# Attention x products as four 64 by 64 TensorE tiles in place of block-diagonal full-array products, two groups per batch

## The chip, the cores and the metric

One Trainium2 chip, one of its cores. The metric is the device time of one execution in microseconds (us): three runs of the kernel before gave 284.06, 284.75 and 286.88, median 284.75. A core has TensorE (PE; its weight loads are listed as PEld), VectorE (DVE), ScalarE (ACT), GpSimd (POOL) and SyncE (SP), which issues most DMAs. Matmuls write PSUM, which ACT and DVE read.

## The reference

Linear attention on q, k, v of shape (8 batches, 8 heads, 576 tokens, 64), then a two-layer network with a snake activation on the 4608 x 512 result:

```python
q_s = exp(q) / sum over d            # per token and head
k_s = exp(k) / sum over tokens       # per head and d
kv  = einsum('bhsd,bhse->bhde', k_s, v)          # 64 x 64 per head
x   = einsum('bhsd,bhde->bhse', q_s, kv)         # -> x: 4608 tokens x 512
h   = x @ w_in                                   # 512 -> 2048
g   = h + sin(alpha * h)**2 / alpha
out = g @ w_out                                  # 2048 -> 512, float32
```

## The kernel before, in words

All matmuls take bf16 operands. The order of every engine's work is written out by hand (`tc.manual_schedule()`, line 54): the program order of the Python is the order on each engine.

**Layout of the attention.** A batch's 576 tokens are 64 partitions by 9 token groups (J = 9, P = 64): token = 9 p + j. A head is (i, e), i = 0..3, e = 0, 1; a tile has partition e*64 + p. The four i are taken as two halves ii (called *head pairs* below; ii holds i = ii and i = ii + 2, which are x = 0 and x = 1). `kv_mm` (line 164) makes kv of a batch with 64 x 64 TensorE tiles: 72 products of 65 columns (the 65th is the sum for the division), 36 per ii; rows are chosen by e, output partitions by x, and e chooses one of two PSUM banks. `kv_norm` (179) divides by the sums and writes `kbd`, a block-diagonal 128 x 128 matrix per (e, ii): x = 0 in the upper left block, x = 1 in the lower right, zeros elsewhere (memset, line 310); that takes two DVE multiplies of 64 partitions. q is normalised by `norm_q` (140) and transposed, by TensorE for batches 0 and 1 and by DMA after that, into `qT`, partition x*64 + d, columns ii, j, e, p.

**x products.** `attn_chunk` (228) and `attn_out` (217) multiply one 128 x 128 block of `kbd` with up to 512 columns of `qT`; the result, c = 2*ii + e, is partitions x*64 + d of xT. Per batch that is 4 blocks of 576 columns. A copy on DVE or ACT brings PSUM to `xT` (SBUF, 128 x 4 x 2560 in bf16, a ring of five token tiles).

**The network.** 4608 tokens are nine *token tiles* t of 512. `mm_h` (247) makes one *h tile* (128 of the 2048 features, 512 tokens): four products of 512 columns over c, into one PSUM bank. There are 16 h tiles, or *slots* ni, per t. `sine` (258) runs the sine on ACT and the square on ACT, POOL or DVE; `combine` (269) adds on DVE, writes G and thereby frees the PSUM bank. `mm_o` (273) makes the output, 64 products of 512 columns per t, accumulated over ni; `evac_o` (283) copies and stores it.

**Order.** Batch 0 fills the start (lines 361 to 401): load, exp, normalise, transpose, kv, x, with the first h products between. Batch 1 is made amid the output products of t = 0 (456 to 504). The ninth token group (j = 8) of batches 0 and 1 comes late: q by `late_q8` (512), transposed after slot 11 and multiplied after slot 15 of t = 1 (eight products of 64 columns). Batch 2 lies amid the output products of t = 1 (549 to 577): four products of 384 columns into banks of the h pools, then the last three groups into a tile of `ps_a`. From t = 2 on, batch b = t + 1 is made in the slots of t by `attn_back` (581): kv at slot 5, then four x steps (of 4 and 5 token groups for each ii) at slots 9, 11, 13, 15; t = 7 and 8 have no attention. kv and x of these batches share one PSUM tile of two banks, `ps_a` with one buffer, so each waits until the copy of the one before has been made. In t >= 3 about 2.6 output products of t - 1 follow every h tile (line 619); ACT does both the sine and the square there, and at the start of every t the exp of q and k of batch t + 1, with two loads of its function tables.

**Weights.** `load_win` (106) loads w_in in pieces with a cast on POOL's DMA queue: partition 64*x + d of chunk c holds row (x, c, d), line 81, in the order in which the x products leave the features.

Of the kernel before, what the change touches and what calls it, by code (L numbers as in the profile page):

```python
# [15 lines left out]
F32 = mybir.dt.float32  # L16
BF16 = mybir.dt.bfloat16
AX = mybir.ActivationFunctionType
ALU = mybir.AluOpType
# [4 lines left out]
def kernel(  # L24
# [20 lines left out]
    J = 9  # L45
    P = S // J
    nN = d_ff // 128
    MF = 512
# [23 lines left out]
    alpha_rows = singles.tile([nN, 128], F32, name="alpha_rows")  # L72
    alpha_sb = singles.tile([128, nN], F32, name="alpha_sb")
    inva_sb = singles.tile([128, nN], F32, name="inva_sb")
    kbd = [singles.tile([128, 2, 2, 128], BF16, name=f"kbd{n}") for n in range(2)]
    vb = [singles.tile([128, J, 4 * 65], BF16, name=f"vb{n}") for n in range(2)]

    def src_view(t, b):
        return t[b].rearrange("(i e) (p j) d -> (e p) i (j d)", e=2, j=J)

    win_v = moe_w_in.rearrange("(x c d) n -> x d c n", x=2, c=4)
    wout_v = moe_w_out.rearrange("(no ni) d -> ni no d", ni=128)
    out_v = out.rearrange("(b p j) d -> b j p d", b=B, j=J)

# [30 lines left out]
    A = {}  # L115
# [48 lines left out]
    def kv_mm(b, ii, pool, split=False):  # L164

        if ii == 0 or split:
            A["kvp", b] = pool.tile([128, 2, 512], F32, name="kvp", tag="a")
        kvp, ke, vt = A["kvp", b], A["ke", b], vb[b % 2]
        for j in range(J):
            for x in range(2):  # L170
                h = 2 * ii + x
                for e in range(2):
                    r = slice(64 * e, 64 * e + 64)
                    nc.tensor.matmul(kvp[64 * x:64 * x + 64, e, ii * 65:(ii + 1) * 65],  # L174
                                     ke[r, j, h * 64:(h + 1) * 64],
                                     vt[r, j, h * 65:(h + 1) * 65],
                                     start=(j == 0), stop=(j == J - 1))
# [12 lines left out]
    def q_tile(b):  # L190
        if ("qT", b) not in A:
# [23 lines left out]
    XO = ((0, 4), (4, 9))  # L215

    def attn_out(b, ii, half, pool, eng):
        qT, kt = A["qT", b], kbd[b % 2]
        j0, j1 = XO[half]
        n = (j1 - j0) * P  # L220
        xp = pool.tile([128, 2, 512], F32, name="xp", tag="a")
        for e in range(2):
            nc.tensor.matmul(xp[:, e, 0:n], kt[:, e, ii], qT[:, ii, j0:j1, e * 64:(e + 1) * 64],  # L223
                             start=True, stop=True)
        c0 = (J * b + j0) * P % NX
        eng(xT[:, 2 * ii:2 * ii + 2, c0:c0 + n], xp[:, :, 0:n])  # L226

    def attn_chunk(b, c, j0, j1, xp):

        ii, e = divmod(c, 2)  # L230
        nc.tensor.matmul(xp, kbd[b % 2][:, e, ii], A["qT", b][:, ii, j0:j1, e * 64:(e + 1) * 64],
                         start=True, stop=True)


    G = {}

# [3 lines left out]
    def bank(kind):  # L240

        if kind == "k":
            return ps_k.tile([128, 2, MF], F32, name="kvp", tag="a")[:, 0]
        pool = {"a": lambda: ps_h[0], "b": lambda: ps_h[1], "l": lambda: ps_l, "o": lambda: ps_o}[kind]()
        return pool.tile([128, MF], F32, name={"l": "lp", "o": "op"}.get(kind, "hp"), tag=kind)

    def mm_h(t, ni, k0=0, k1=4):

        if ni == 0 and k0 == 0:
            G[t] = gpool.tile([128, nN, MF], BF16, name="g")  # L250
        hp = HP[t, ni] if k0 else bank(BANKS.get(t, 4 * "aabb")[ni])
        HP[t, ni] = hp
        for ki in range(k0, k1):
            nc.tensor.matmul(hp, win[:, ki, ni * 128:(ni + 1) * 128],  # L254
                             xT[:, ki, t * MF % NX:t * MF % NX + MF], start=(ki == 0), stop=(ki == 3))
        return hp

    def sine(t, ni, hp, sq):
# [122 lines left out]
    cast_v0(1, 5, 9, DVE_CP)  # L381

    xp = [bank("b") for _ in range(2)]
    for c in range(2):
        attn_chunk(0, c, 0, 8, xp[c])
    DVE_CP(xT[:, 0, 0:MF], xp[0])
    ACT_CP(xT[:, 1, 0:MF], xp[1])
# [4 lines left out]
    for ki in range(2):  # L392
        for ni in range(2):
            mm_h(0, ni, ki, ki + 1)
    for c in range(2, 4):
        xp = bank("l")
        attn_chunk(0, c, 0, 8, xp)
        DVE_CP(xT[:, c, 0:MF], xp)
    for ki in range(2):
        for ni in range(2, 4):  # L400
            mm_h(0, ni, ki, ki + 1)
# [21 lines left out]
    def take(it, n=1000):  # L423
        for _ in range(n):
            if next(it, 0) == 0:
                return
# [4 lines left out]
    with ES:  # L431
# [47 lines left out]

        def x_half(ii):  # L480
            xp = [bank("a") for _ in range(2)]
            for e in range(2):
                attn_chunk(1, 2 * ii + e, 0, 8, xp[e])
            for e in range(2):
                (ACT_CP, DVE_CP)[e](xT[:, 2 * ii + e, MF:2 * MF], xp[e])

        kv_mm(1, 0, ps_k, split=True)
        kv_norm(1, 0, 1)
# [23 lines left out]
        def late_q8(ni):  # L512
            if ni == 11:
                tp = ps_k.tile([128, 2, 2, 128], BF16, name="tp", tag="a")
                for b in range(2):
                    for ii in range(2):
                        nc.tensor.transpose(tp[:, ii, b], A["qe", 1][:, J - 2 + b, ii * 128:(ii + 1) * 128], identb)
                DVE_CP(A["qT", 1][:, :, J - 2:J], tp)
            elif ni == 15:
                xp = ps_k.tile([128, 4, 2, P], F32, name="xp", tag="a")  # L520
                for c in range(4):
                    ii, e = divmod(c, 2)
                    for b in range(2):
                        nc.tensor.matmul(xp[:, c, b], kbd[b][:, e, ii],
                                         A["qT", 1][:, ii, J - 2 + b, e * 64:(e + 1) * 64], start=True, stop=True)
                DVE_CP(xT[:, :, 16 * P:18 * P], xp.rearrange("p c b n -> p c (b n)"))

        for ni in range(nN):
            h_slot(1, ni, SQ[ni], lag)
# [33 lines left out]
    norm_q(3, [GP])  # L563
    take(os, 20)

    c0 = J * 2 * P
# [6 lines left out]
    for c in range(4):  # L573
        attn_chunk(2, c, 6, 9, xp[:, c // 2, (c % 2) * 3 * P:(c % 2 + 1) * 3 * P])
    DVE_CP(xT[:, :, c0 + 6 * P:c0 + 9 * P].rearrange("p (h c) n -> p h c n", h=2),
           xp.rearrange("p h (c n) -> p h c n", c=2))
    take(os)
    q_transpose_dma(3)
    load_batch(4)

    def attn_back(b, n, engs=4 * (DVE_CP,), xs=(4, 6, 8, 10)):
        if n == 0:
            kv_mm(b, 0, ps_a)
            kv_mm(b, 1, ps_a)
            kv_norm(b)
        elif n in xs:
            m = xs.index(n)
            attn_out(b, m // 2, m % 2, ps_a, engs[m])

    SQ2 = "PAPPAPAPPAPAPPAP"  # L590
    for ni in range(nN):
        h_slot(2, ni, SQ2[ni], lag)
        flush(lag, 2)
        attn_back(3, ni - 5, (DVE_CP, ACT_CP, ACT_CP, DVE_CP), (4, 6, 8, 10))
    flush(lag, 0)

    for t in range(3, nT):
        b = t + 1 if t + 1 < B else None
        os = o_stream(t - 1)
        done = 0  # L600
        if b is not None:

            exp_q(b)
            exp_k(b)
            cast_v(b, [GP_CP, GP_CP])
            norm_q(b, [GP])
            take(os, 8)
            done = 8
        for ni in range(nN):
# [12 lines left out]
        take(os)  # L622
# [36 lines left out]
```

## Time and profile before

| | |
|---|---|
| median of three runs | 284.75 us |
| the profiled execution's own time | 283.85 us |
| its span, first to last instruction | 282.1 us |
| mean granted TensorE clock | 0.997 |
| PE busy | 270.1 us, 1826 matmuls recorded |
| ACT, DVE, POOL busy | 225.5, 188.7, 83.8 us |
| h products, L254 (into hp) | 127.9 us busy, x507 |
| output products, L274 (into op) | 121.6 us busy, x477 |
| kv products, L174 | 6.8 us busy, x576 |
| x products, L223 (batches 3 to 7) | 8.2 us busy, x40 |
| xT copies, L226 on DVE | 13.5 us busy, x18 |
| kbd multiplies, L187 on DVE | 7.4 us busy, x20 |

The profile is of one execution. Busy time of PE is a union of modelled intervals: a matmul's listed duration (379 ns for 512 columns) is from its start to its last result, and the next one starts before that. So the distance between starts is the price of a matmul in a stream, not its duration. A few matmul records are missing. "Idle before, releaser" after the bar in a line says how long the engine stood before these instructions and what ended it.

### The profile page before, as it was taken

Reading aid. Unit: us, or ns where it says so; the run is one execution under the profiler, and the core shown is the slowest. Engines: PE = TensorE matmul, PEld = TensorE weight load, DVE = VectorE, ACT = ScalarE, POOL = GpSimd, SP = SyncE. Lnnn points to the kernel's source line nnn. Section 1 sums busy time; section 2 is a strip of 40 time slices with the busy share of each in tenths; the row PEclk is TensorE's granted clock in tenths of the full one; section 3 lists DMA queues with packets and bytes.
Section 4 is the critical chain, followed back from the end, with each engine's and each line's share of the span. In section 5 each row is a group of like instructions: output and inputs, shape, how many; then the busy total and the mean of one; then the engine's idle time right before and its main releaser. Section 6 shows DMA issues by size and latency. Waiting matters only on the chain.

```text
span 282.1 us, 4812 instructions
## 1 busy us (share of the span) xinstructions
PE 270.1 (96%) x1826; PEld 128.0 (45%) x1855; DVE 188.7 (67%) x288; ACT 225.5 (80%) x322; POOL 83.8 (30%) x80
## 2 busy tenths in 40 slices
PE   1999999999999999999999999999999999999994
PEld 0444444444444444444444444444444444444443
DVE  3968768899967768766875677567775555555412
ACT  3989576999589999899989998999877777777400
POOL 1988421877676550115003500340000000000000
PEclk9999999999999999999999999999999999999998
DMA  7999999996599039811992099109011111111143
GB/s 252 310 173 221 280 332 322 358 345 243 124 224 393 10 68 329 305 37 38 266 386 50 22 283 388 27 18 160 6 34 37 37 40 37 37 38 43 42 104 74
DMA packets 39127, 45.80 MB, mean 162 GB/s; under 512 B 17072, under 2 KB 22464, under 8 KB 39104
## 3 DMA queue, kind: packets, MB, share of 16 engines
q1 hardware_dynamic: 33360, 40.57, 46.9%
q0 software_dynamic: 5552, 4.79, 10.4%
q8 instruction: 14, 0.23, 0.3%
q10 hardware_dynamic: 192, 0.14, 0.2%
q14 instruction: 9, 0.07, 0.1%
HBM read 36.71 MB, written 9.44 MB: 164 GB/s over the span
## 4 chain that ended last, share of the span: by engine, by line
PE 84%; DMA 6%; ACT 3%; DVE 2%; POOL 1%; issue 1%; SPq 1%; ACTq 0%
PE op L274 38%; PE hp L254 37%; DMA st_v<-in_v_dram 6%; PE xp L223 2%; PE kvp L174 2%; PE lp L254 2%; POOL s L264 1%; PE op L629 1%; PE op L254 1%; ACT s L260 1%; PE kvp L254 1%; ACT vb L329 1%; DVE g L270 1%; SPq L299 1%; SPq L445 0%
## 5 line engine op out<-in xcount | busy, mean ns | idle before, releaser
L270 DVE SCALAR_TENSOR_TENSOR g<-s,inva_sb,hp 128x512 bf16<-128x512 f32 x128 | 94.1, 745 | 58.1 <-ACT s L262 52.6
L254 PE MATMUL hp<-xT,win 128*128 128x512 bf16 x507 | 127.9, 379 | 0.4
L274 PE MATMUL op<-wout,g 128*128 128x512 bf16 x477 | 121.6, 379 | 1.4 <-issue 0.6
L260 ACT ACTIVATE s<-hp,alpha_sb 128x512 f32<-128x512 f32 x128 | 86.3, 682 | 22.9 <-PE hp L254 21.2
L254 PEld LDWEIGHTS <-win 128*128 128x128 bf16 x576 | 56.0, 98 | 67.5 <-issue 1.3
L274 PEld LDWEIGHTS <-g 128*128 128x128 bf16 x560 | 54.0, 98 | 61.0 <-DVE g L270 0.3
L262 ACT ACTIVATE s<-s 128x512 f32<-128x512 f32 x112 | 70.5, 630 | 3.5
L264 POOL TENSOR_TENSOR s<-s 128x512 f32<-128x512 f32 x29 | 30.4, 1063 | 20.0 <-ACT s L260 19.9
L153 POOL TENSOR_TENSOR qn<-qe,qs 128x1152 bf16<-128x1152 bf16 (+1 forms) x12 | 25.1, 2109 | 34.1 <-DVE qs L147 22.7
L286 DVE COPY o<-op 128x512 f32<-128x512 f32 (+2 forms) x33 | 22.1, 668 | 9.9 <-PE op L274 5.5
L138 POOL CAST vb<-st_v 128x1152 bf16<-128x1152 f32 x12 | 14.7, 1257 | 45.3 <-DMA st_v<-in_v_dram 45.3
L119 ACT ACTIVATE qe<-st_q 128x1152 bf16<-128x1152 f32 (+2 forms) x18 | 17.7, 1025 | 6.7 <-DMA st_q<-in_q_dram 6.6
L119 ACT ACTIVATE ke<-st_k 128x1152 bf16<-128x1152 f32 x16 | 17.9, 1151 | 1.2 <-DMA st_k<-in_k_dram 1.2
L146 DVE TENSOR_REDUCE qs<-qe 128x36 f32<-128x2304 bf16 x5 | 12.8, 2553 | 7.9 <-ACT qe L119 7.9
L226 DVE CAST xT<-xp 128x512 bf16<-128x512 f32 (+1 forms) x18 | 13.5, 749 | 0.0
L119 ACT ACT_TABLE_LOAD x7 | 9.0, 1283 | 1.3 <-PEq L643 1.2
L274 PE MATMUL lp<-wout,g 128*128 128x512 bf16 x31 | 8.8, 379 | 0.2 <-issue 0.2
L274 PE MATMUL hp<-wout,g 128*128 128x512 bf16 x30 | 8.6, 379 | 0.1
L223 PE MATMUL xp<-qT,kbd 128*128 128x256 bf16 (+1 forms) x40 | 8.2, 286 | 0.0
L174 PEld LDWEIGHTS <-ke 64*64 64x64 bf16 x576 | 5.8, 108 | 4.6 <-ACT ke L119 0.8
L187 DVE TENSOR_TENSOR kbd<-kvp,kvr 64x256 bf16<-64x256 f32 (+1 forms) x20 | 7.4, 369 | 0.5
L254 PE MATMUL lp<-xT,win 128*128 128x512 bf16 x30 | 7.5, 379 | 0.1
(86 smaller groups left out, 135.0 us busy)
## 6 DMA issues: line engine op xcount, KB each, us to landing
out_dram<-o SPq DMA_DIRECT2D x70, 128.0 KB, 2.4
st_q<-in_q_dram SPq DMA_DIRECT2D x6, 1152.0 KB, 6.7
st_k<-in_k_dram SPq DMA_DIRECT2D x6, 1152.0 KB, 8.8
st_v<-in_v_dram SPq DMA_DIRECT2D x6, 1152.0 KB, 11.4
st_k<-in_k_dram SPq DMA_DIRECT2D x4, 576.0 KB, 7.5
st_q<-in_q_dram SPq DMA_DIRECT2D x4, 512.0 KB, 6.1
st_v<-in_v_dram SPq DMA_DIRECT2D x3, 576.0 KB, 8.0
wout<-in_moe_w_out_dram POOLq DMA_DIRECT2D x3, 512.0 KB, 10.3
```

What stands on the lines that cost most here:

```text
L119: nc.scalar.activation(dst[:, :, ii * 128:(ii + 1) * 128].rearrange("p j (x d) -> p x j d", x=2), src[:, ii::2], AX.Exp)
L138: engs[ii](vv[:, 2 * ii:2 * ii + 2, :, 0:D], staged["v", b][:, ii::2])
L153: engs[ii % len(engs)].tensor_tensor(qn[:, ii, 0:j1].rearrange("p j (x d) -> p j x d", x=2), qe[:, ii], part.unsqueeze(3).to_broadcast([12 ...
L223: nc.tensor.matmul(xp[:, e, 0:n], kt[:, e, ii], qT[:, ii, j0:j1, e * 64:(e + 1) * 64], start=True, stop=True)
L226: eng(xT[:, 2 * ii:2 * ii + 2, c0:c0 + n], xp[:, :, 0:n])
L254: nc.tensor.matmul(hp, win[:, ki, ni * 128:(ni + 1) * 128], xT[:, ki, t * MF % NX:t * MF % NX + MF], start=(ki == 0), stop=(ki == 3))
L260: nc.scalar.activation(s, hp, AX.Sin, scale=alpha_sb[:, ni:ni + 1])
L262: nc.scalar.activation(s, s, AX.Square)
L264: nc.gpsimd.tensor_tensor(s, s, s, op=ALU.mult)
L270: nc.vector.scalar_tensor_tensor(G[t][:, ni], in0=s, scalar=inva_sb[:, ni:ni + 1], in1=hp, op0=ALU.mult, op1=ALU.add)
L274: nc.tensor.matmul(acc, G[t][:, ni, j * 128:(j + 1) * 128], wout[:, ni, :], start=(ni == 0), stop=(ni == nN - 1))
L286: eng(o[:, cols], acc)
```

## The change

The x products become 64 x 64 TensorE tiles, as the kv products are. `kbd` loses its zero blocks: [128, 2, 2, 64], partition x*64 + d, then (e, ii), then the 64 columns of kv; one DVE multiply of 128 partitions fills what two of 64 did, and the memset goes. `attn_x` issues four products for one ii: rows x*64 of `qT` and `kbd`, output partitions e*64, and x chooses the PSUM bank. A result chunk is now c = 2*x + ii, with e inside the chunk, so w_in is read in its plain order of rows, (c, e, d), and `mm_h` takes its chunks in the order `KO` = 0, 2, 1, 3, that is ii = 0 first.

The columns are dealt out otherwise too. A batch's x products are one group of four with 512 columns for each ii (j = 0 to 7), at slots 9 and 13 from t = 2 on, each followed by two copies of 512 columns (`x_copy`, which splits where the ring of xT wraps: for batch 4 at 256). The ninth token group is made by `last_j`, eight products of 64 columns: from batch 3 on right behind the kv products of the next batch and into the free columns of that PSUM tile; for batch 2 with its second group, and for batch 7 by itself at slot 15 of t = 6, into a `ps_a` tile.

```diff
-    kbd = [singles.tile([128, 2, 2, 128], BF16, name=f"kbd{n}") for n in range(2)]
+    kbd = [singles.tile([128, 2, 2, D], BF16, name=f"kbd{n}") for n in range(2)]
-    win_v = moe_w_in.rearrange("(x c d) n -> x d c n", x=2, c=4)
+    win_v = moe_w_in.rearrange("(c x d) n -> x d c n", x=2, c=4)
...
-        for x in range(2):
-            r = slice(64 * x, 64 * x + 64)
-            nc.vector.tensor_tensor(kt[r, :, i0:i1, r], src[r, :, :, 0:D],
-                                    kvr[r].unsqueeze(3).to_broadcast([64, 2, m, D]), op=ALU.mult)
+        nc.vector.tensor_tensor(kt[:, :, i0:i1], src[:, :, :, 0:D],
+                                kvr.unsqueeze(3).to_broadcast([128, 2, m, D]), op=ALU.mult)
...
+    def attn_x(b, ii, j0, j1, outs):
+        for e in range(2):
+            for x in range(2):
+                r = slice(64 * x, 64 * x + 64)
+                nc.tensor.matmul(outs[x][64 * e:64 * e + 64], kbd[b % 2][r, e, ii],
+                                 A["qT", b][r, ii, j0:j1, e * 64:(e + 1) * 64], start=True, stop=True)
+    def x_copy(eng, c, b, xp):
+        n0 = min(8 * P, NX - J * b * P % NX)
+        for n, m in ((0, n0), (n0, 8 * P)):
+            if n < m:
+                d0 = (J * b * P + n) % NX
+                eng(xT[:, c, d0:d0 + m - n], xp[:, n:m])
+    def last_j(b, xn):
+        for ii in range(2):
+            attn_x(b, ii, J - 1, J, [xn[:, x, ii * P:(ii + 1) * P] for x in range(2)])
+    def last_j_copy(b, xn):
+        DVE_CP(xT[:, :, x_cols(b, J - 1, J)].rearrange("p (x i) n -> p x i n", x=2),
+               xn[:, :, 0:2 * P].rearrange("p x (i n) -> p x i n", i=2))
+    KO = (0, 2, 1, 3)
...
-        for ki in range(k0, k1):
-            nc.tensor.matmul(hp, win[:, ki, ni * 128:(ni + 1) * 128],
-                             xT[:, ki, t * MF % NX:t * MF % NX + MF], start=(ki == 0), stop=(ki == 3))
+        for k in range(k0, k1):
+            nc.tensor.matmul(hp, win[:, KO[k], ni * 128:(ni + 1) * 128],
+                             xT[:, KO[k], t * MF % NX:t * MF % NX + MF], start=(k == 0), stop=(k == 3))
...
-        nc.vector.memset(kbd[n], 0.0)
...
-    for c in range(4):
-        xp = bank("aabb"[c])[:, 0:6 * P]
-        attn_chunk(2, c, 0, 6, xp)
-        (ACT_CP, DVE_CP)[c % 2](xT[:, c, c0:c0 + 6 * P], xp)
-        take(os, 3 if c == 1 else 1)
-    xp = ps_a.tile([128, 2, 512], F32, name="xp", tag="a")[:, :, 0:6 * P]
-    for c in range(4):
-        attn_chunk(2, c, 6, 9, xp[:, c // 2, (c % 2) * 3 * P:(c % 2 + 1) * 3 * P])
-    DVE_CP(xT[:, :, c0 + 6 * P:c0 + 9 * P].rearrange("p (h c) n -> p h c n", h=2),
-           xp.rearrange("p h (c n) -> p h c n", c=2))
+    for ii in range(2):
+        xp = [bank("ab"[ii]) for _ in range(2)]
+        attn_x(2, ii, 0, 8, xp)
+        if ii == 1:
+            xn = ps_a.tile([128, 2, 512], F32, name="xp", tag="a")
+            last_j(2, xn)
+        for x in range(2):
+            x_copy((ACT_CP, DVE_CP)[x], 2 * x + ii, 2, xp[x])
+        take(os, 4)
+    last_j_copy(2, xn)
...
-    def attn_back(b, n, engs=4 * (DVE_CP,), xs=(4, 6, 8, 10)):
-        if n == 0:
-            kv_mm(b, 0, ps_a)
-            kv_mm(b, 1, ps_a)
-            kv_norm(b)
-        elif n in xs:
-            m = xs.index(n)
-            attn_out(b, m // 2, m % 2, ps_a, engs[m])
+    def x_pair(b, ii, xp, engs):
+        attn_x(b, ii, 0, 8, xp)
+        for x in range(2):
+            x_copy(engs[x], 2 * x + ii, b, xp[x])
+    def attn_kv(b):
+        kv_mm(b, 0, ps_a)
+        kv_mm(b, 1, ps_a)
+        if b > 3:
+            xn = A["kvp", b][:, :, 256:512]
+            last_j(b - 1, xn)
+        kv_norm(b)
+        if b > 3:
+            last_j_copy(b - 1, xn)
...
-        attn_back(3, ni - 5, (DVE_CP, ACT_CP, ACT_CP, DVE_CP), (4, 6, 8, 10))
+        if ni == 5:
+            attn_kv(3)
+        elif ni in (9, 13):
+            x_pair(3, ni // 12, pair(), (DVE_CP, ACT_CP))
...
-                attn_back(b, ni - 5)
+                if ni == 5:
+                    attn_kv(b)
+                elif ni in (9, 13):
+                    x_pair(b, ni // 12, pair(), 2 * (DVE_CP,))
+                if b == B - 1 and ni == 15:
+                    xn = ps_a.tile([128, 2, 512], F32, name="xp", tag="a")
+                    last_j(b, xn)
+                    last_j_copy(b, xn)
```

Batches 0 and 1 use `attn_x` in the same places as `attn_chunk` before, and the ninth groups of these two after slot 15 of t = 1 become sixteen 64 x 64 products of 64 columns. `pair()` takes a two-bank tile of `ps_a`.

More of the change, by code (lines that the diff above doesn't have):

```diff
@@ L213, in q_transpose_dma, with x_cols @@
             nc.sync.dma_start(out=out, in_=in_, transpose=True)
[L215 to L221, printed above, removed]
-        for e in range(2):
-            nc.tensor.matmul(xp[:, e, 0:n], kt[:, e, ii], qT[:, ii, j0:j1, e * 64:(e + 1) * 64],
-                             start=True, stop=True)
-        c0 = (J * b + j0) * P % NX
[L226 to L232, printed above, removed]
+    def attn_x(b, ii, j0, j1, outs):
+        for e in range(2):
+            for x in range(2):
+                r = slice(64 * x, 64 * x + 64)
+                nc.tensor.matmul(outs[x][64 * e:64 * e + 64], kbd[b % 2][r, e, ii],
+                                 A["qT", b][r, ii, j0:j1, e * 64:(e + 1) * 64], start=True, stop=True)
+    def x_cols(b, j0, j1):
+        c0 = (J * b + j0) * P % NX
+        return slice(c0, c0 + (j1 - j0) * P)
+    def x_copy(eng, c, b, xp):
[11 more added lines that the diff above has]
+    KO = (0, 2, 1, 3)
     G = {}
@@ L383 @@
     xp = [bank("b") for _ in range(2)]
-    for c in range(2):
-        attn_chunk(0, c, 0, 8, xp[c])
+    attn_x(0, 0, 0, 8, xp)
     DVE_CP(xT[:, 0, 0:MF], xp[0])
-    ACT_CP(xT[:, 1, 0:MF], xp[1])
+    ACT_CP(xT[:, 2, 0:MF], xp[1])
     ACT_CP(A["qT", 0][:, 1, 0:8], tp1)
@@ L394 @@
             mm_h(0, ni, ki, ki + 1)
[L395 to L398, printed above, removed]
+    xp = [bank("l") for _ in range(2)]
+    attn_x(0, 1, 0, 8, xp)
+    for x in range(2):
+        DVE_CP(xT[:, 2 * x + 1, 0:MF], xp[x])
     for ki in range(2):
@@ L481, in x_half @@
             xp = [bank("a") for _ in range(2)]
[L482 to L485, printed above, removed]
+            attn_x(1, ii, 0, 8, xp)
+            for x in range(2):
+                (ACT_CP, DVE_CP)[x](xT[:, 2 * x + ii, MF:2 * MF], xp[x])
         kv_mm(1, 0, ps_k, split=True)
@@ L519, in late_q8 @@
             elif ni == 15:
-                xp = ps_k.tile([128, 4, 2, P], F32, name="xp", tag="a")
-                for c in range(4):
-                    ii, e = divmod(c, 2)
+                xp = ps_k.tile([128, 2, 512], F32, name="xp", tag="a")
+                for ii in range(2):
                     for b in range(2):
-                        nc.tensor.matmul(xp[:, c, b], kbd[b][:, e, ii],
-                                         A["qT", 1][:, ii, J - 2 + b, e * 64:(e + 1) * 64], start=True, stop=True)
-                DVE_CP(xT[:, :, 16 * P:18 * P], xp.rearrange("p c b n -> p c (b n)"))
+                        for e in range(2):
+                            for x in range(2):
+                                r, c = slice(64 * x, 64 * x + 64), (2 * ii + b) * P
+                                nc.tensor.matmul(xp[64 * e:64 * e + 64, x, c:c + P], kbd[b][r, e, ii],
+                                                 A["qT", 1][r, ii, J - 2 + b, e * 64:(e + 1) * 64],
+                                                 start=True, stop=True)
+                DVE_CP(xT[:, :, 16 * P:18 * P].rearrange("p (x i) n -> p x i n", x=2),
+                       xp[:, :, 0:4 * P].rearrange("p x (i n) -> p x i n", i=2))
         for ni in range(nN):
@@ L564 @@
     take(os, 20)
-    c0 = J * 2 * P
-    for c in range(4):
-        xp = bank("aabb"[c])[:, 0:6 * P]
-        attn_chunk(2, c, 0, 6, xp)
-        (ACT_CP, DVE_CP)[c % 2](xT[:, c, c0:c0 + 6 * P], xp)
-        take(os, 3 if c == 1 else 1)
-    xp = ps_a.tile([128, 2, 512], F32, name="xp", tag="a")[:, :, 0:6 * P]
-    for c in range(4):
-        attn_chunk(2, c, 6, 9, xp[:, c // 2, (c % 2) * 3 * P:(c % 2 + 1) * 3 * P])
-    DVE_CP(xT[:, :, c0 + 6 * P:c0 + 9 * P].rearrange("p (h c) n -> p h c n", h=2),
-           xp.rearrange("p h (c n) -> p h c n", c=2))
+    for ii in range(2):
+        xp = [bank("ab"[ii]) for _ in range(2)]
[3 more added lines that the diff above has]
+            last_j(2, xn)
+        for x in range(2):
+            x_copy((ACT_CP, DVE_CP)[x], 2 * x + ii, 2, xp[x])
+        take(os, 4)
+    last_j_copy(2, xn)
     take(os)
@@ L579, with pair @@
     load_batch(4)
-    def attn_back(b, n, engs=4 * (DVE_CP,), xs=(4, 6, 8, 10)):
-        if n == 0:
-            kv_mm(b, 0, ps_a)
-            kv_mm(b, 1, ps_a)
-            kv_norm(b)
-        elif n in xs:
-            m = xs.index(n)
-            attn_out(b, m // 2, m % 2, ps_a, engs[m])
+    def x_pair(b, ii, xp, engs):
+        attn_x(b, ii, 0, 8, xp)
+        for x in range(2):
+            x_copy(engs[x], 2 * x + ii, b, xp[x])
+    def pair():
+        t = ps_a.tile([128, 2, 512], F32, name="xp", tag="a")
+        return [t[:, x] for x in range(2)]
+    def attn_kv(b):
[7 more added lines that the diff above has]
+            last_j_copy(b - 1, xn)
     SQ2 = "PAPPAPAPPAPAPPAP"
```

## The prediction

> **What bounds the kernel now.** I read the engine sums first, then the table of stretches, then the groups by shape, and last the timeline around the two kinds of attention work on TensorE.
>
> ```profile
> PE 270.1 (96%) x1826; PEld 128.0 (45%) x1855; DVE 188.7 (67%) x288; ACT 225.5 (80%) x322; POOL 83.8 (30%) x80
> ```
>
> PE is the bound. The stretches (each engine's busy us and instruction count) say where:
>
> ```profile
> 0.00:16.00 16.00, 9.81 (x111) 4.71 (x113) 10.32 (x26) 11.33 (x14) 9.91 (x21) 1.00 0.99 267
> 46.00:60.00 14.00, 13.95 (x75) 6.54 (x74) 12.06 (x20) 13.34 (x23) 9.50 (x9) 1.00 0.98 348
> 92.00:101.90 9.90, 9.85 (x47) 4.46 (x47) 6.55 (x8) 9.78 (x12) 5.75 (x5) 1.00 0.01 4
> 120.00:208.00 88.00, 87.21 (x616) 41.59 (x623) 61.50 (x87) 81.88 (x115) 17.99 (x11) 1.00 0.49 137
> ```
>
> PE (first pair) idles only before 16 us; after that it is full in every stretch at a granted clock of 1.00. So the change is worth what it takes off the PE stream, except where another engine is just as full: ACT (fourth pair) is busy 9.78 of 9.90 us in 92 to 101.9. What is in the stream, by shape (count | busy us, mean ns):
>
> ```profile
> L254 PE MATMUL hp<-xT,win 128*128 128x512 bf16 x507 | 127.9, 379 | 0.4
> L174 PE MATMUL kvp<-vb,ke 64*64 64x65 bf16 x576 | 6.8, 196 | 0.3 <-ACT vb L329 0.3
> L223 PE MATMUL xp<-qT,kbd 128*128 128x320 bf16 x20 | 4.3, 299 | 0.0
> L223 PE MATMUL xp<-qT,kbd 128*128 128x256 bf16 x20 | 3.8, 272 | 0.0
> ```
>
> 379 ns is latency; what counts is start to start. Two pieces of timeline give it (start, us). The x products of half a token set, now:
>
> ```profile
> 113.53 0.59 PE L254 MATMUL hp<-xT,win 128*128 128x512 bf16 x2
> 113.96 0.43 PE L223 MATMUL xp<-qT,kbd 128*128 128x320 bf16 x2
> 114.23 0.59 PE L274 MATMUL op<-wout,g 128*128 128x512 bf16 x2
> ```
>
> Two 512-column products take 113.53 to 113.96, so 0.216 us each (0.42 ns a column), and two of 320 columns take 0.27: a full-array product costs its columns and nothing else. The same at 110.94 to 111.16 for 256 columns, 0.22. Now 64 by 64 tiles, which the kernel already has in the kv products:
>
> ```profile
> 80.25 0.81 PE L254 MATMUL op<-xT,win 128*128 128x512 bf16 x3
> 80.99 0.81 PE L174 MATMUL kvp<-vb,ke 64*64 64x65 bf16 x72
> 81.73 0.39 PE L254 MATMUL hp<-xT,win 128*128 128x512 bf16 x1
> ```
>
> and, in a narrow look at its end, the last four of them:
>
> ```profile
> 81.56 0.24 PE L174 MATMUL kvp<-vb,ke 64*64 64x65 bf16 x4
> 81.73 0.39 PE L254 MATMUL hp<-xT,win 128*128 128x512 bf16 x1
> ```
>
> Three readings. Rate: a block of 36 (42.83 to the next start at 43.24) takes 0.41 us, this one of 72 takes 0.74, so nine groups of four cost 0.33: 37 ns a group of 65 columns. One tile alone would need 65 x 0.42 = 27 ns, so four do run abreast. Way in: three 512-column products end their turn at 80.25 + 3 x 0.216 = 80.90, yet the first 64 by 64 starts at 80.99: 0.09 lost. Way out: the 36-block's nine groups are worth 0.33, but it takes 0.41: 0.08 lost to a slower first group and the way out, and the narrow look puts it there (from the last group's start at 81.56 to 81.73 is 0.17, of which some 0.06 are staggered columns). **Every visit to the 64 by 64 shape costs 0.17 to 0.22 us on top of its columns.** Before, the only visits are those for kv.
>
> **The change part by part.**
>
> *x products.* Per batch now: 2 x (0.22 + 0.27) = 0.98 us. After: per head pair one group of four 64 by 64 products of 512 columns. Its price is not in the trace, so from the kv rows: 0.09 in, 0.03 for the staggered start and the first loads (the first group of a block is that much slower), 0.216 for the columns, 0.08 to 0.11 out: 0.44. Bounds: 0.22, were the visit free (the full-array pair shows no such cost), and 0.51, if it streams at kv's 37 ns per 65 columns (0.29) with 0.22 of visit. I take 0.44, because kv is the only row in that shape. Against 0.49 that wins 0.05 a head pair, not half.
>
> *Ninth group.* It rides on the next kv block: two more groups of four in a block that has been entered, 2 x 0.033 to 0.037 = 0.07. A batch thus costs 2 x 0.44 + 0.07 = 0.95 against 0.98.
>
> Here the Trainium skill can be weighed. "TensorEngine Tiling (Array Packing)", section Theoretical Speedup, gives up to 2x for each dimension of at most 64; used on block diagonals, half of whose array holds zeros, it would halve 0.49 to 0.25 a head pair, an estimate worth some 2.9 us over batches 2 to 7 if all of it reached the end. Its Key Properties say that a change of tiling mode drains the engine, without a price; the rows above price it at 0.2 us a visit, which leaves nearly nothing of the 2.9.
>
> *Where it reaches the end*, in order:
> - Start, batch 0: 0. The second x pair at 14.58 waits for ACT's copy of qT (13.51 to 14.53), and PE's next wait is the second xT copy on DVE (15.01, 1.29 for two), so PE goes on at 16.35 as before. The missing memsets of kbd (2 x 0.27 on DVE at 2 us) and one kbd multiply fewer (0.29) lie beside these.
> - Batch 1, 41 to 45.6: the x pair at 44.55 waited 0.22 for kbd on DVE, whose second half (0.29) goes; PE gains about 0.2. ACT there gains only 0.04 (its copy at 44.32 waits for an output product), and at 60 PE waits for DVE:
>
> ```profile
> 59.30 0.73 DVE L270 SCALAR_TENSOR_TENSOR g<-s,inva_sb,lp 128x512 bf16<-128x512 f32 x1
> 60.08 0.59 PE L274 MATMUL op<-wout,g 128*128 128x512 bf16 x2
> ```
>
>   The output product needs that PSUM bank, and starts 0.05 after its release. DVE runs behind a full ACT (46 to 57). So -0.04 is credited. The two ninth groups before it (8 x 0.029 now; 4 groups and a visit after) are in that shadow too.
> - Batch 2: -0.03. Its copies on DVE are 512 wide (0.68) where they were 384 (0.55), before the first h tile of token tile 2, which needs them in the order 0, 2, 1, 3. DVE comes to them at 74.72, and two in a row take 0.61 + 0.69 (the two at 15.01), to 76.02; the last is due at 75.7 + 3 x 0.216 = 76.3. Covered, by 0.3.
> - Batch 3, in token tile 2: 0.88 against 0.98, -0.10 (its ninth group comes with kv 4). Also a wait goes: pairs two slots apart shared one PSUM tile.
>
> ```profile
> 86.55 0.68 DVE L226 CAST xT<-xp 128x512 bf16<-128x512 f32 x1
> 87.28 0.43 PE L223 MATMUL xp<-qT,kbd 128*128 128x320 bf16 x2
> ```
>
>   PE stood 0.14 here and 0.05 at 89.32. Four slots apart (some 3.5 us) nothing waits. Together -0.29, but at the fifth h tile of token tile 3 stands
>
> ```profile
> 101.07 0.75 DVE L270 SCALAR_TENSOR_TENSOR g<-s,inva_sb,hp 128x512 bf16<-128x512 f32 x1 [1.80 <-ACT s L262]
> 101.89 0.59 PE L254 MATMUL hp<-xT,win 128*128 128x512 bf16 x2
> ```
>
>   again PE 0.07 behind the bank's release, behind an ACT full since 85.4. ACT gains what PE has gained by 82.8, where ACT still waits 0.49 for PE (0.07), and its two xT copies (0.67 and 0.59, after 2 x 0.59: 0.09). Up to 101.9 I credit 0.17, not 0.36.
> - Batches 4 to 6: 3 x -0.03 = -0.09. The slots there have slack: the bank for a later slot is free 1.5 to 2.9 us ahead, more than the 0.7 by which the doubled DVE copies (2 x 0.68 in a row, 4 x about 0.4 for batch 4, whose columns wrap) delay one combine. DVE's sum hardly moves: 2 x 0.68 + 2 x 0.82 + 2 x 0.42 before, 4 x 0.68 + 0.42 + about 0.4 after.
> - Batch 7 has no next kv: its ninth group makes a visit of its own at slot 15, 0.2 + 2 x 0.04 = 0.29, so 0.95 + 0.29 - 0.98 = +0.26. It waits for the PSUM tile of the pair two slots (3 us) ahead, whose copies take 2 x 0.68 on DVE after one combine: by my count free about 1 us before.
> - w_in: the same number and size of transfers, other rows; the order of head pairs in h (0, 2, 1, 3) follows the copies. Both queues, SP and POOL, keep their order: 0.
>
> Sum: -0.17 - 0.09 + 0.26 = 0.00. The profiled execution took 283.85 (span 282.1 and 1.75 around it), 0.9 under the median of 284.75. The sum moves neither: 283.85 for such an execution, **284.75** for the median.
>
> **The rivals.**
> - *The visit is free for long products* (only short ones show it): 0.22 a head pair. For: it is a price per visit, and kv has 65-column products only. Against: the way in follows a 512-column product and is paid all the same, ten blocks out of ten. After 101.9: batches 4 to 6 at 0.44 + 0.07, -0.47 each, batch 7 about -0.40, and 0.17 before: -2.0, 282.8.
> - *Four tiles don't stay abreast over 512 columns*: the slower side. The place is the x group, with four moving streams of 512 columns. Two at a time: 0.44 + 0.22 = 0.66 a pair; batches 2, 4, 5, 6 each 1.32 + 0.13 - 0.98 = +0.47, batch 3 +0.34 - 0.19, batch 7 +0.83: +2.9, 287.6. One at a time: 0.44 + 0.65 = 1.09, some +8.5, 293. It decides as soon as a pair costs more than 0.44 to 0.46, since the sum is nothing there, and reaches 1% at about 0.66. Against: 37 ns for four where two at a time need 54.
> - *Doubled copies hold a PSUM bank*: in token tile 3 a combine at slot 9 is 0.9 later behind four narrow copies (4 x 0.4 for 0.68); it costs only beyond the slack of 2.9 there or 1.5 at slot 5, so 0 to 0.5: 285.2 at most.
> - *Nothing measurable*, which is my forecast, though the change does what it says.
>
> **How the numbers follow.** Forecast 0.80; visit free 0.05; not abreast 0.08 (two thirds two at a time); bank held 0.07. The likeliest case's own range is 283.9 to 286.0: its terms from -0.3 (a pair at 0.41) to +0.7 (0.51 on twelve pairs, less the 0.2 that the waits had hidden), and half a us of run to run, since three runs span 284.06 to 286.88. The range goes on from there towards both outer cases, 283.2 to 286.6. A measurement of this kernel can tell about 1% (2.8 us) from no change. Faster by that much needs more than the free visit: 0.03. Slower by that much is half of two at a time and all of one at a time, and a little for what I don't see: 0.08. Within: 0.89.
>
> **What would show it.** Right: L254 to the group and back 0.65 to 0.68 from the last full start to the next full start (0.216 + 0.44); four 64 by 64 products starting within 0.02 of each other; the kv blocks 0.07 longer; no wait at 87 and 89; one visit of 0.29 at the end of token tile 6; PE dense after 16 us. Wrong: if a group takes under 0.35 or over 0.55, if PE shows idle time before an h tile in token tiles 3 to 6, or if the waits at 60.1 and 101.9 give way, which would let 0.2 more through at each.

## The result, and the profile after

The kernel with the change took 285.61 us (median of 22 runs, 285.05 to 287.94), the kernel before 284.24 (22 runs, 283.65 to 286.88). The ratio is 1.0048, 95% interval 1.0032 to 1.0064: about 1.4 us slower, small, but clear of the noise. The forecast was no change, 284.75 in 283.2 to 286.6; the median lies in that range, but the loss itself was not forecast. The profiled execution took 285.55, with a span of 283.8 where the kernel before had 282.1.

The engine sums of the kernel after (busy us, share of the span, instructions):

```profile
PE 269.8 (95%) x1890; PEld 124.0 (44%) x1919; DVE 184.1 (65%) x285; ACT 225.1 (79%) x322; POOL 83.5 (29%) x80
```

Beside the line of before: PE has 0.3 us less to do, DVE 4.6 less, ACT 0.4 less, and the span is 1.7 longer. No engine got more work. Somebody waits. The group of the h products in the kernel after says who; the number behind the second bar is the idle time ahead of these products, then its releaser and that releaser's part:

```profile
L263 PE MATMUL hp<-xT,win 128*128 128x512 bf16 x506 | 127.5, 379 | 1.4 <-DVE g L279 0.7
```

Before, this idle time was 0.4. The waits of PE between the first h tile of token tile 2 and the fifth of token tile 3 (76 to 104 us), line by line with total, times and longest, after:

```profile
PE hp L263 <- DVE g L279: 0.7, 1, 0.7
PE op L283 <- DVE g L279: 0.5, 1, 0.5
```

The same view of the kernel before lists none there (it leaves out waits as short as the 0.14 and 0.05 that the prediction named). `DVE g L279` is the combine, which writes G for the output products and frees the PSUM bank of its h tile. To see where in the run that happens, take the distances between the starts of chosen h tiles in the two traces. "t2" is the first h tile of token tile 2, "t3+4" the fifth of token tile 3, and so on; each stretch from t3+4 on holds all of one batch's attention (batch 4 up to batch 7), and the first holds batch 3's.

| us between starts | start to t2 | t2 to t3+4 | to t4+4 | to t5+4 | to t6+4 | to t7+4 | sum, t2 to t7+4 |
|---|---|---|---|---|---|---|---|
| before | 75.72 | 26.17 | 29.02 | 29.45 | 29.42 | 26.40 | 140.46 |
| after | 75.80 | 27.46 | 29.10 | 29.42 | 29.40 | 26.67 | 142.04 |
| difference | +0.08 | **+1.29** | +0.08 | -0.03 | -0.02 | +0.27 | +1.58 |
| predicted | -0.07 | -0.10 | -0.03 | -0.03 | -0.03 | +0.26 | +0.07 |

The prediction's 0.17 up to t3+4 holds 0.07 that it expects ahead of t2 (batches 1 and 2), so 0.10 are left for the stretch with batch 3. From t7+4 to the end both take 65.9. So nearly the whole loss lies in one stretch, the one with batch 3, and there the sign of the prediction was wrong. Here are the places that answer to the lines at 101.07 and 101.89 of before, in the timeline of the kernel after (start, duration, then idle before and its releaser):

```profile
102.46 0.75 DVE L279 SCALAR_TENSOR_TENSOR g<-s,inva_sb,hp 128x512 bf16<-128x512 f32 x1 [1.81 <-ACT s L271]
103.26 0.81 PE L263 MATMUL hp<-xT,win 128*128 128x512 bf16 x3 [0.74 <-DVE g L279]
```

The combine still comes when ACT's square is done, but 1.39 later on the clock (0.08 of it from the later start of t2). PE did not stand here before: the 0.07 from the bank's release to its start at 101.89 is no wait, since its products lie 0.216 apart there, and a start that does wait comes 0.05 behind the release. Now PE stands 0.74. So ACT itself has become late. ACT's only new releaser in the view of waits, 82 to 102 us:

```profile
ACT xT L231 <- DVE xT L231: 1.3, 2, 0.8
```

and the two places in its timeline:

```profile
86.19 0.63 ACT L271 ACTIVATE s<-s 128x512 f32<-128x512 f32 x1
87.34 0.58 ACT L231 CAST xT<-xp 128x512 bf16<-128x512 f32 x1 [0.52 <-DVE xT L231]
...
91.71 0.58 ACT L231 CAST xT<-xp 128x512 bf16<-128x512 f32 x1 [0.80 <-DVE xT L231]
92.19 0.69 ACT L269 ACTIVATE s<-hp,alpha_sb 128x512 f32<-128x512 f32 x1
...
94.14 1.28 ACT L119 ACT_TABLE_LOAD   x1
```

In the kernel before, ACT comes to the same table load here:

```profile
92.76 1.28 ACT L119 ACT_TABLE_LOAD   x1
```

DVE's copies of the other half of the same x group, from the timeline of DVE:

```profile
86.63 0.68 DVE L231 CAST xT<-xp 128x512 bf16<-128x512 f32 x1
...
91.00 0.68 DVE L231 CAST xT<-xp 128x512 bf16<-128x512 f32 x1
```

The first ends at 87.31 and ACT's copy starts at 87.34; the second ends at 91.68, ACT's starts at 91.71. ACT finishes token tile 2 and comes to its table load at 94.14 instead of 92.76. Those 1.38 are nearly the two waits, 0.52 + 0.80 = 1.32. ACT is full from there on (8.24 of the 8.32 us up to 102.46), so they travel with it to the next places where PE needs its work: the bank at 103.26, and before that the last part of G of token tile 2, whose combine comes behind ACT's sine and POOL's square:

```profile
96.08 1.25 PE L283 MATMUL op<-wout,g 128*128 128x512 bf16 x5 [0.47 <-DVE g L279]
```

The 0.47 and 0.74 are counted from the modelled end of the product before. From start to start, less the 0.216 that a product costs, PE loses 0.64 and 0.91 there, 1.55 together; the stretch grew by only 1.29, because PE has less to do in it and the small waits at 87 and 89 are gone. The reading so far: **each half of a batch 3 x group is copied by another engine (DVE one, ACT the other), out of one PSUM tile of two banks, and ACT's copy does not start until DVE's has ended.**

The rest of the change did what the prediction said. An x group of the kernel after, in the stream:

```profile
111.93 0.59 PE L263 MATMUL hp<-xT,win 128*128 128x512 bf16 x2
112.46 0.41 PE L218 MATMUL xp<-qT,kbd 64*64 64x512 bf16 x4
112.80 0.60 PE L283 MATMUL op<-wout,g 128*128 128x512 bf16 x2
```

The last full product starts at 111.93 + 0.22 = 112.15; the group 0.31 behind it, the next output product 0.34 behind the group. In the raw starts: 309 ns from the last full product to the group (216 for the product, 93 lost), the four 64 by 64 products at 0, 3, 7 and 10 ns, 342 ns from the group to the next full product, and 10 ns by which the product after that is late: 0.093 + 0.342 + 0.010 = 0.445.

### The profile page after: what moved, and what is told of

The parts are those of the page before. It is cut to its first block, busy times and chain, and to the rows that moved or that the text cites. A ratio compares the mean times of both kernels' runs of the same rounds, so it can differ in the third digit from the quotient of the medians.

```text
span 283.8 us, 4934 instructions
## 1 busy us (share of the span) xinstructions
PE 269.8 (95%) x1890; PEld 124.0 (44%) x1919; DVE 184.1 (65%) x285; ACT 225.1 (79%) x322; POOL 83.5 (29%) x80
## 4 chain that ended last, share of the span: by engine, by line
PE 83%; ACT 5%; DMA 4%; DVE 3%; issue 2%; POOL 2%; SPq 0%; ACTq 0%
PE op L283 35%; PE hp L263 34%; PE hp L283 3%; PE lp L263 2%; PE lp L283 2%; DMA st_k<-in_k_dram 2%; DMA st_v<-in_v_dram 2%; ACT s L269 2%; PE kvp L174 2%; DVE g L279 2%; POOL s L273 1%; PE op L659 1%; PE kvp L263 1%; PE xp L218 1%; ACT ke L119 1%
## 5 line engine op out<-in xcount | busy, mean ns | idle before, releaser
L279 DVE SCALAR_TENSOR_TENSOR g<-s,inva_sb,hp 128x512 bf16<-128x512 f32 x128 | 94.3, 744 | 60.8 <-ACT s L271 54.5
L283 PEld LDWEIGHTS <-g 128*128 128x128 bf16 x560 | 52.8, 98 | 64.7 <-issue 2.5
L231 DVE CAST xT<-xp 128x512 bf16<-128x512 f32 (+1 forms) x22 | 11.9, 584 | 0.0
L174 PE MATMUL kvp<-vb,ke 64*64 64x65 bf16 x576 | 6.9, 196 | 0.7 <-ACT vb L337 0.7
L109 POOL DMA_DIRECT2D win<-in_moe_w_in_dram x12 | 7.4, 656 | 0.4 <-DMA st_v<-in_v_dram 0.4
```

The costliest lines, as they stand in the source:

```text
L279: nc.vector.scalar_tensor_tensor(G[t][:, ni], in0=s, scalar=inva_sb[:, ni:ni + 1], in1=hp, op0=ALU.mult, op1=ALU.add)
L283: nc.tensor.matmul(acc, G[t][:, ni, j * 128:(j + 1) * 128], wout[:, ni, :], start=(ni == 0), stop=(ni == nN - 1))
```

## The experiments

The theory (T in the texts on record): ACT's copy waits for DVE's because both read one PSUM tile, and in that stretch ACT sets the pace. Its rivals: the 64 by 64 shape and its visits cost more at the end than the group shows (V); the loss comes with the x pairs as they now lie, with their places and banks, whoever copies first (P); or, about the size of the terms, a visit is hidden and free at the end (F). Ratios are against the kernel before, run beside them on the same chip (283.48 and 283.47 us there), from 6 or 12 runs of each version. The kernel with the change was not run again beside them; its 1.0048 is from the result above.

**ACT's copy first.**

```diff
-            x_pair(3, ni // 12, pair(), (DVE_CP, ACT_CP))
+            x_pair(3, ni // 12, pair(), (ACT_CP, DVE_CP))
```

> The changed kernel, with the two copies of each x group of batch 3 dealt out the other way: ACT first, then DVE. Theory T (tied copies): both halves lie in one two-bank PSUM tile, and the second copy waits for the first; in the changed kernel ACT's copy stood 0.52 and 0.80 us for DVE's, in a stretch in which ACT sets the pace, and that made the kernel slower by 1.4. With ACT first it is DVE that waits, which has idle time there: ACT's two waits go, the fifth h tile of token tile 3 starts about 1.35 us earlier than in the changed kernel (near 101.9), and the time is 284.2 to 284.4, a ratio to the kernel before of 1.000 (0.998 to 1.002). Rival V (the visits to the 64 by 64 shape cost more at the end than 0.445 a group in the stream): nothing changes, 1.005. Rival P (what hurts is that ACT's copies lie at slots 9 and 13 instead of 11 and 13, not that they wait): 1.003 to 1.005.

283.36 us, ratio 0.9997 (0.9987 to 1.0006). t2 to t3+4 takes 25.94 instead of 27.46. The same dependency is there, turned round. The DVE timeline of this kernel:

```profile
86.51 0.69 DVE L231 CAST xT<-xp 128x512 bf16<-128x512 f32 x1 [0.62 <-ACT xT L231]
```

Now DVE waits 0.62 for ACT, and it costs nothing, since in this stretch DVE has the time. The work, the engines, the slots and the shape are those of the change; swapping two names takes the loss away. Neither the shape nor the place of the groups is the cause.

**Both copies on DVE.**

```diff
-            x_pair(3, ni // 12, pair(), (DVE_CP, ACT_CP))
+            x_pair(3, ni // 12, pair(), (DVE_CP, DVE_CP))
```

> The changed kernel, with both copies of batch 3's x groups on DVE. T: ACT has neither the waits (1.32) nor the copies (2 x 0.585) in that stretch, so it is 2.5 us earlier at token tile 3, more than PE can use; PE gains 1.36 and then some 0.2 to 0.35 that ACT had held back: 283.9 to 284.1, ratio 0.999 (0.997 to 1.001). V: 1.005. P: like T, so this run alone doesn't part T from P.

283.37, ratio 0.9998 (0.9988 to 1.0008). t2 to t3+4 again 25.94: 0.23 below the kernel before. That is the gain of batch 3, which ACT's wait had covered; the prediction had credited some 0.10 of it.

**The change's order with full-array products.** Block-diagonal `kbd`, two 128 by 128 products a group, w_in's old rows; groups, slots, ninth groups and copies as after.

```diff
-    kbd = [singles.tile([128, 2, 2, D], BF16, name=f"kbd{n}") for n in range(2)]
+    kbd = [singles.tile([128, 2, 2, 128], BF16, name=f"kbd{n}") for n in range(2)]
...
         for e in range(2):
-            for x in range(2):
-                r = slice(64 * x, 64 * x + 64)
-                nc.tensor.matmul(outs[x][64 * e:64 * e + 64], kbd[b % 2][r, e, ii],
-                                 A["qT", b][r, ii, j0:j1, e * 64:(e + 1) * 64], start=True, stop=True)
+            nc.tensor.matmul(outs[e], kbd[b % 2][:, e, ii],
+                             A["qT", b][:, ii, j0:j1, e * 64:(e + 1) * 64], start=True, stop=True)
...
```

> The changed kernel's order of work (two groups a batch, ninth token group with the next kv, the same copies on the same engines) with the old full-array products on block-diagonal kbd, so no visit to the 64 by 64 shape but for kv. T: ACT waits as in the changed kernel, so the time stays near 285.4 (ratio 1.003 to 1.005); the TensorE stream itself is 0.1 to 0.2 shorter after token tile 3, most of it at batch 7. V: back to 284.2, ratio 1.000.

285.34, ratio 1.0062 (1.005 to 1.0073): as slow as the change, with no x product on 64 by 64 tiles. That is a little above the 1.003 to 1.005 expected; the interval overlaps with that of the change. Its waits of ACT and PE in the same stretch:

```profile
ACT xT L231 <- DVE xT L231: 1.3, 2, 0.8
```

```profile
PE hp L263 <- DVE g L279: 0.7, 1, 0.7
PE op L283 <- DVE g L279: 0.5, 1, 0.5
```

The same two lines as in the kernel after, to the tenth. The loss is there without the shape.

**The same, both copies on DVE.** This sets the two shapes side by side without the wait.

```diff
-            x_pair(3, ni // 12, pair(), (DVE_CP, ACT_CP))
+            x_pair(3, ni // 12, pair(), (DVE_CP, DVE_CP))
```

> The full-array version of the run before, with both copies of batch 3 on DVE. T: 283.8 to 284.0, 0.1 under the 64 by 64 version with the same copies, because a group costs 0.432 against 0.445 and batch 7's lone ninth group 0.12 against 0.29, while the ninth group with kv costs 0.12 against 0.08; ratio 0.998 to 1.000. V: the same as the full-array version with the old copies, and clearly (by 1.4) below the 64 by 64 version on DVE.

283.40, ratio 0.9995 (0.9985 to 1.0004). From t2 to t7+4 it takes 140.41, the 64 by 64 version with the same copies 140.52. In times the two cannot be told apart, and in the stages the small tiles are 0.12 behind: 0.15 in batch 7, whose ninth group pays a visit of its own (26.67 against 26.52), less 0.03 in the others together. The 64 by 64 tiles bring nothing here.

**Two tiles of one bank.** For batch 3, the pool of the two-bank tile is closed at slot 9 and its two banks are dealt out as two tiles; everything else is as after, DVE first.

```diff
-    ps_a = ctx.enter_context(tc.tile_pool(name="ps_a", bufs=1, space=PSUM, reuse_waits="tile"))
+    AS = ExitStack()
+    ps_a = AS.enter_context(tc.tile_pool(name="ps_a", bufs=1, space=PSUM, reuse_waits="tile"))
...
         elif ni in (9, 13):
-            x_pair(3, ni // 12, pair(), (DVE_CP, ACT_CP))
+            if ni == 9:
+                AS.close()
+                ps_x = AS.enter_context(tc.tile_pool(name="ps_x", bufs=2, space=PSUM, reuse_waits="tile"))
+            two = [ps_x.tile([128, 512], F32, name="xp", tag="x") for _ in range(2)]
+            x_pair(3, ni // 12, two, (DVE_CP, ACT_CP))
     flush(lag, 0)
+    AS.close()
+    ps_a = ctx.enter_context(tc.tile_pool(name="ps_a", bufs=1, space=PSUM, reuse_waits="tile"))
```

> The changed kernel, but batch 3's x groups go into two one-bank PSUM tiles in the same two banks, instead of the halves of one two-bank tile; engines, order and slots of the copies stay as in the changed kernel (DVE first, then ACT). Theory T (the second copy waits because both halves are one tile): neither copy waits for the other, ACT's 0.52 and 0.80 us go, and the time comes down to the kernel before, ratio 1.000 (0.998 to 1.002). Rival O (the wait is one of order: an ACT copy issued after a DVE copy into the same x buffer, or too early for ACT): it stays at 1.005.

283.52, ratio 1.0002 (0.999 to 1.0014). Timelines of this kernel, DVE and then ACT:

```profile
86.85 0.68 DVE L231 CAST xT<-xp 128x512 bf16<-128x512 f32 x1
...
90.59 0.68 DVE L231 CAST xT<-xp 128x512 bf16<-128x512 f32 x1
```

```profile
86.95 0.57 ACT L231 CAST xT<-xp 128x512 bf16<-128x512 f32 x1
...
90.40 0.58 ACT L231 CAST xT<-xp 128x512 bf16<-128x512 f32 x1
...
92.85 1.28 ACT L119 ACT_TABLE_LOAD   x1
```

Both copies run at once, each as long as it was alone, and t2 to t3+4 takes 25.95. This run settles the cause: same products, same order, same engines, same banks (the other pools hold the other six), and only the count of tiles differs. What makes ACT wait is the semaphore between the two readers of one PSUM tile, not the banks or the ports, and not `xT`, which both copies write here too. (The Trainium skill, page "PSUM — Partial Sum Buffer", section "PSUM bank collisions raise a hardware error", wants two engines guarded against each other in one bank, reads against reads included, and holds that accesses to different banks run clean. This run agrees with the second half: two banks, two readers, no wait and no loss. The wait of the change is coarser than that rule, since the two halves lay in different banks all along.)

**Six more visits.** Starting from the version with both copies on DVE, the x groups of batches 4 to 6 are cut into two of 256 columns with an output product between them.

```diff
-                    x_pair(b, ni // 12, pair(), 2 * (DVE_CP,))
+                    if b < B - 1:
+                        xp = pair()
+                        attn_x(b, ni // 12, 0, 4, [o[:, 0:4 * P] for o in xp])
+                        take(os, 1)
+                        done += 1
+                        attn_x(b, ni // 12, 4, 8, [o[:, 4 * P:8 * P] for o in xp])
+                        for x in range(2):
+                            x_copy(DVE_CP, 2 * x + ni // 12, b, xp[x])
+                    else:
+                        x_pair(b, ni // 12, pair(), 2 * (DVE_CP,))
```

> The version with both copies of batch 3 on DVE, with each x group of batches 4 to 6 split in two of 256 columns, and one output product between them: six visits to the 64 by 64 shape more, the same columns. By the stream's price (a visit of four times 512 columns 0.445, so four times 256 some 0.34, twice 0.68) each costs 0.23 more: 6 x 0.23 = 1.4 us, ratio 1.0045 to 1.005 against the 0.9998 of the unsplit one. Rival F (a visit is free or nearly so at the end, since other engines have slack there): 1.000.

284.84, ratio 1.0052 (1.0039 to 1.0064). Above the version that it was made from that is 0.54%, some 1.5 us, or 0.25 a visit; in the stages the three batches take 0.47, 0.47 and 0.46 more, 0.23 a visit. In its timeline:

```profile
116.75 0.30 PE L218 MATMUL xp<-qT,kbd 64*64 64x256 bf16 x4
116.98 0.39 PE L283 MATMUL op<-wout,g 128*128 128x512 bf16 x1
117.30 0.30 PE L218 MATMUL xp<-qT,kbd 64*64 64x256 bf16 x4
```

A group of 256 columns holds PE for 0.23 before the next full product, though its columns are worth 0.108 (half of 0.216), and the group after that starts 0.32 behind a product worth 0.22: 0.12 out and 0.10 in. In these three batches a visit is paid in full at the end; none of it is hidden.

**The kernel before, with its copies tied.** If one tile for two engines is the cause, the kernel before must get slower when its second and third step of batch 3 are copied half by DVE and half by ACT, instead of whole by ACT.

```diff
-        eng(xT[:, 2 * ii:2 * ii + 2, c0:c0 + n], xp[:, :, 0:n])
+        if eng is None:
+            DVE_CP(xT[:, 2 * ii, c0:c0 + n], xp[:, 0, 0:n])
+            ACT_CP(xT[:, 2 * ii + 1, c0:c0 + n], xp[:, 1, 0:n])
+        else:
+            eng(xT[:, 2 * ii:2 * ii + 2, c0:c0 + n], xp[:, :, 0:n])
...
-        attn_back(3, ni - 5, (DVE_CP, ACT_CP, ACT_CP, DVE_CP), (4, 6, 8, 10))
+        attn_back(3, ni - 5, (DVE_CP, None, None, DVE_CP), (4, 6, 8, 10))
```

> The kernel before, full-array products and four x steps, but the copies of batch 3's second and third x step are halved: DVE takes one half of the PSUM tile, ACT the other, where ACT took both. ACT has 0.6 us less to copy. T: ACT's halves now wait for DVE's, which stand behind combines: some 0.4 and 1.4 us; ACT is some 1.2 later at token tile 3, and the time rises by 1.0 to 1.5 us, ratio 1.0035 to 1.005. Rival O or V: ACT is a little earlier and nothing is lost, 0.999 to 1.000.

283.82, ratio 1.0016 (1.0003 to 1.003): at most slightly slower, and far from the 1.0035 to 1.005 expected. Timelines, ACT and then PE:

```profile
89.92 0.43 ACT L228 CAST xT<-xp 128x320 bf16<-128x320 f32 x1 [0.29 <-DVE xT L227]
...
91.57 0.37 ACT L228 CAST xT<-xp 128x256 bf16<-128x256 f32 x1
```

```profile
90.39 0.38 PE L223 MATMUL xp<-qT,kbd 128*128 128x256 bf16 x2
```

The tie is there: the first copy waited 0.29 for DVE. At the second, DVE had come to its half in time. The way by which T expected the loss is not there: ACT also has less to copy (0.43 + 0.37 where it had 0.67 + 0.59), and at the fifth h tile of token tile 3 PE doesn't wait for the bank (it starts 0.11 behind the release, in a dense stream). From t2 to t3+4 it still takes 0.14 more, and the starts of PE's products say where: the x step at 90.39 waits 0.18 for the shared PSUM tile, where the same step before (89.32) waited 0.05, since ACT's copy, which frees the tile, ends at 90.35 behind its own wait. From t2 to t7+4 the whole difference is 0.14; what the median shows beyond that (0.35 in all) is not found in the trace. So this run bears out that such copies are tied, and not what the tie costs where ACT sets the pace.

None of the versions beats the kernel before by more than its interval; 0.9995, 0.9997, 0.9998 and 1.0002 are all the same time.

## Why the prediction was right or wrong

- **Batch 3: the step that failed.** The prediction put ACT's two copies there at their busy time, "after 2 x 0.59: 0.09" of gain, and credited 0.17 up to the fifth h tile of token tile 3, some 0.10 of it in the stretch with batch 3. The stretch became 1.29 longer. The two copies wait 0.52 and 0.80 for DVE's copies out of the same tile. The prediction had itself shown that ACT is full in this stretch (9.78 of 9.90 us) and sets the bank's release at 101.89, so it held everything needed to price a wait on ACT; it did not ask whether one was added. "Four slots apart (some 3.5 us) nothing waits" looked only at PE and the next group, and never at the two copies of one group. What the step is worth without the wait is shown by the versions that take the wait away: -0.23 and -0.22, twice the credit. Idle time of PE before an h tile in token tile 3 stood among the prediction's signs of being wrong, and it is there. That 285.61 lies inside the stated range is luck: what widened the range upwards were other things, a dearer x group, the scatter of the runs, tiles that do not stay abreast and banks held by copies.
- **The x group: right.** 0.44 predicted, 0.445 measured, in 0.093 and out 0.126 beyond 10 ns of stagger and 0.216 of columns. Two terms were off and made up for each other: the stagger (0.03 predicted) and the way out (0.08 to 0.11). That the way in "follows a 512-column product and is paid all the same, ten blocks out of ten", holds for the seven kv blocks of the kernel before that do follow a full 512-column product (308 to 310 ns each); the other three follow something else. The rivals that lived on this number (a free visit at 0.22; tiles that do not stay abreast, 0.66 or 1.09) are out by the trace alone, and the six added visits show that the price also reaches the end.
- **Ninth group with the next kv: right.** The block of 72 + 8 products took 0.066 more in the kernel after (1.002 against 0.936 us for batches 6 and 7, from its start to the next matmul recorded, one record missing in both); predicted 0.07. By itself, for batch 7, it takes 0.29, as predicted:

```profile
208.70 1.03 PE L263 MATMUL hp<-xT,win 128*128 128x512 bf16 x4
209.66 0.26 PE L218 MATMUL xp<-qT,kbd 64*64 64x64 bf16 x8
209.85 1.25 PE L283 MATMUL op<-wout,g 128*128 128x512 bf16 x5
```

  The fourth full product starts at 208.70 + 3 x 0.216 = 209.35, so the group comes 0.10 after that product's turn is over, and holds PE for 0.19.
- **Batches 5 to 7: right**, -0.03, -0.02 and +0.27 for -0.03, -0.03 and +0.26. The doubled DVE copies held no bank that PE needed.
- **Batch 4: off by 0.11** (+0.08 for -0.03). Every version with the new slots has it, the full-array ones too (29.10 to 29.12, the run with six more visits left aside, against 29.02, and 29.01 in the tied kernel before), so it comes with the order and not with the shape. The trace shows the way: ahead of slot 14's h tile now lie two x groups (0.89) and the ninth group (0.07), where 0.71 of x products lay, which is 0.25 more. Slot 14's h tile starts 16.26 behind t3+4 instead of 16.01, ACT, which waits for it, comes to its table load 19.98 behind instead of 19.74, and the combine that frees the bank for t4+4 is 0.25 later too. PE starts that h tile 53 ns behind the release (218 before) and loses 0.11 there.
- **The waits at 87 and 89: right**, they are gone, though only the versions without ACT's wait show what that is worth.
- **The start: right within what can be told.** The first h tile of token tile 2 starts anywhere from 74.98 to 76.65 in the nine profiles, whose code up to there is nearly the same; a difference of 0.08 says nothing.
- **The rule.** The Trainium skill, page "TensorEngine Tiling (Array Packing)", promises up to 2x a dimension (Theoretical Speedup), and says that a change of mode drains the engine (Key Properties). The trace shows four tiles that run at full rate for 512 columns, starting within 10 ns, as the first would have it, and a loss at each change of shape, as the second would. With that loss the group takes 0.445, where the full-array pair costs 2 x 0.216 = 0.432 by itself.

With the four copies of batch 3 as they were costed, the sum of zero would have been about right (0.9997, 0.9998 and 1.0002 were measured without ACT's wait). The mistake was one missing question in the one place where the other engine was full.

## What to carry to other kernels

When one tile's copy is split between two engines, ask who reads first, whether a tile shared by both makes the second reader wait, and which of the two sets the pace there: put that engine first, or give each a tile of its own. A move of work between engines has to be priced with the waits it ties, in each stretch by the engine that is full there, and a busy time is only the lower end of that. And a small-tile product pays for entering and leaving its shape, so put it beside other products of that shape, or leave it in a full array.

## What the runs showed of the hardware

- Entering the 64 by 64 shape behind a full 512-column product costs 0.09 us (308 to 310 ns from start to start, 216 of them the product), the same before products of 64, 65, 256 or 512 columns. Leaving it costs 0.13 behind four products of 256 or 512 columns and 0.11 behind four of 64. Four products with four moving streams of 512 columns start 3, 7 and 10 ns behind the first and run at one full-array product's pace.
- DVE and ACT read two neighbouring PSUM banks at once with no loss when the banks are two tiles: 0.68 and 0.57 us, as long as alone.
